# Expert 0's second 128 rows: half of their product before the attention branch ends, half behind it

## The chip, the cores and the metric

The kernel runs on one core of one Trainium2 chip. The metric is device time in microseconds of one execution. The kernel before takes 646.89 us (median of three runs, 646.09 to 647.37).

## The reference

Three stages follow each other, all in float32. `_attn_ref` is cut to its result, since the change touches only how its output is handed on.

```python
def reference(**kwargs):
    attn_out = _attn_ref(**attn_kwargs)             # B, H, S, D = 2, 8, 768, 64: local and global keys, ALiBi
    x = attn_out.transpose(0, 2, 1, 3).reshape(B, S, H * D)
    x = _moe_ref(x=x, **moe_kwargs)
    return _moe2_ref(x=x, **moe2_kwargs)

def _moe_ref(x, w_gate, w_local, w1, w2):           # E = 8 experts, D = 512, F = 1024
    logits = np.einsum('bsd,de->bse', x, w_gate)
    local_gate = 1.0 / (1.0 + np.exp(-np.einsum('bsd,de->bse', x, w_local).squeeze(-1)))
    for b in range(B):
        prev_e = -1
        for s in range(S):
            fresh_e = int(np.argmax(logits[b, s]))
            e = fresh_e if s == 0 or local_gate[b, s] < 0.5 else prev_e   # else: the expert of the token before
            prev_e = e
            p = softmax(logits[b, s])
            out[b, s] = p[e] * (np.maximum(x[b, s] @ w1[e], 0.0) @ w2[e])

def _moe2_ref(x, w_ch1, w_ch2):                     # FFT over sequence and channels, layer norm, a ReLU layer pair
    ...
```

## The kernel before, in words

**Stages.** The program runs attention and routing (to about 124 us), the eight experts (to about 318), and the mixer (FFT and a ReLU layer pair). Attention has two arms of one branch on the data (`tc.If(fast > 0)`): the fast arm runs here, and the code of the other, longer arm lies behind it, so that every engine jumps over it at the branch's end.

**Products in two halves.** TensorE takes each float32 operand as a high part (`h`, rounded) and the residual (`l`); a product is the sum of three: high by high, high by low, low by high. ScalarE makes the high part and VectorE the residual. A layer of 128 rows is 24 matmuls of 512 columns.

**Attention** goes over six tiles of 128 positions, four units each. `step(k)` runs between the parts of a unit; it takes one step of each background generator and, by the table `AHEAD`, some steps of the early product. `k` counts from the last unit, so `k >= 0` is the tail, in which only outputs and routing are left.

**Routing** (`Route.run`, one generator for each tile) finds each token's expert: `gn` and `gf` (line 528 and 534) are turned by TensorE, a scan carries the expert along (`ex`, line 552), a second scan counts (`cu`, line 561), `rk` (577) and `pos` (589) are the token's place. Then SP's queue writes the tokens to `xs` and GpSimd scatters their numbers to `list`, where each expert has its own part. Two `yield from to(...)` set at which part of a unit a step is taken; the last tile has none, so its steps follow `step(k)` one by one.

**The early product.** After the third tile (`first`), `less` pads expert 0's count to 128, so that the first 128 places of its list are settled; its entries are read (line 604) and its rows gathered to `x0` (607). `early` (862) is a generator that runs the two layers for these 128 rows (chunk 0) in the tail of attention: transposes of `x0` (868), first layer (882), copies of the sums to `hs` (885), `turned` (887: transposes, relu, residual), second layer (898), scaling (913). Its operands `xe`, `he` lie in a weight place (slot 4), its sums in the last raw place.

**The experts.** `Ring` holds four raw places, each for a piece of 1 MB, and six slots for their two halves; `take` splits a piece and loads the next one into its raw place. `Ring.shade` sets the order of the pieces: for each expert the next expert's four (`e`), and eight mixer pieces (`d`) in between, each decoded by VectorE in four instructions. `Moe.run` (1359) begins behind the branch: entries and rows of expert 0's other two chunks (1 and 2), the write of chunk 0's result, the counts (1371), 6 + 6 + 3 matmuls on a zero tile (`WARM`), the transposes of the two chunks. `expert(0)` then runs the first layer on 256 rows at once (`first256`, line 1201) and the second layer on each 128 (`second`, 1181). Chunk 0 of every other expert is part of its own 256 rows.

Of the kernel before, what the change touches and what calls it, by code (L numbers as in the profile page):

```python
# [60 lines left out]
def fast_attention(tc, st, io, route):  # L61
# [4 lines left out]
    with ExitStack() as ctx:  # L66
# [68 lines left out]
        def rowmin(n):  # L135
# [3 lines left out]
            for k in range(2):  # L139
                for j in range(2):  # L140
                    x = 2 * k + j
                    V.tensor_tensor_reduce(  # L142
                        out=u.t[:, x, :u.W], in0=u.sp[:, j, k, :u.W], in1=bias[:, 4 * u.g + x, u.b0:u.b0 + u.W],
                        scale=-0.125, scalar=3.0e38, op0=ALU.add, op1=ALU.min,
                        accum_out=u.nm[:, x:x + 1])
# [62 lines left out]
        bias = res.tile([P, H, 384], F32, name="bias")  # L208
# [44 lines left out]
        kept = []  # L253

        def spare():
            if not kept:
                kept.append(ps_s.tile([P, 2, 2, 256], F32, name="sp"))
            return kept[0]

        def places():  # L260
            for n in range(6):
                if n == 1:
                    yield spare()[:, 0].rearrange("p u n -> p (u n)")
                elif n in (2, 4):
# [4 lines left out]
        ahead = early(nc, st, places())  # L269

        def step(k):
# [13 lines left out]
            if k in SPIN:  # L285
                keep_busy(nc, st, spare()[:, 1].rearrange("p u n -> p (u n)"), SPIN[k])
# [62 lines left out]
def general_attention(tc, st, io, route):  # L349
# [3 lines left out]
    with ExitStack() as ctx:  # L353
# [74 lines left out]
        for _ in early(nc, st, (ps_s.tile([P, 1024], F32, name="sp")[:, :DM] if n in (2, 4) else ps_o.tile([P, DM], F32, name="op") for n in range(6))):  # L428
            pass
# [20 lines left out]
class Route:  # L450
# [31 lines left out]
    def run(self, i, xs, parts=None):  # L482
# [85 lines left out]
        if first:  # L568
# [6 lines left out]
        if soon:  # L575
            yield from to(1)
# [3 lines left out]
        yield from to(3, 2)  # L580
# [9 lines left out]
        for b in range(B):  # L590
            r = (i * B + b) * P
            nc.sync.dma_start(st.xs[r:r + P], xs[b])
            w = G.indirect_dma_start(
# [4 lines left out]
        if first:  # L598

            V.tensor_scalar(su[:1, 0], less, 0.0, None, op0=ALU.max)  # L600
            V.tensor_tensor(cu[:1, P - 1:], cu[:1, P - 1:], su[:1, 0], op=ALU.add)
            for _ in range(EARLY_READ):
                yield
            nc.sync.dma_start(st.ent0, st.list[1:P + 1])
            for _ in range(EARLY_GATHER):
                yield
            G.indirect_dma_start(
                out=st.x0, out_offset=None, in_=st.xs[:(i + 1) * B * P], in_offset=bass.IndirectOffsetOnAxis(ap=st.ent0[:, 0:1], axis=0),
                bounds_check=(i + 1) * B * P - 1, oob_is_err=False)
        if i == NT - 1:  # L610
            yield from self.counts()

# [42 lines left out]
EARLY_READ = 7  # L655
EARLY_GATHER = 6
# [3 lines left out]
WARM = 6, 6, 3  # L660
LOAD = 6
CASTS = (5, 6, 7, 8)
RESTS = (24, 25, 26, 27)
# [1202 lines left out]
```

## Time and profile before

| | |
|---|---|
| median of three runs | 646.89 us (646.09 to 647.37) |
| the profiled execution, in all | 645.5 us |
| its span, first to last instruction | 643.7 us |
| mean granted TensorE clock | 0.995 |
| TensorE busy (matmul) | 622.1 us, 97% of the span |
| VectorE busy | 391.7 us, 61% |
| ScalarE busy | 276.3 us, 43% |
| first product of expert 0's 256 rows | 129.86 us |
| first product of expert 1 | 153.30 us |

The profile calls the engines PE (TensorE), DVE (VectorE), ACT (ScalarE), POOL (GpSimd) and SP. Times in it are microseconds from the span's start. A share of busy time is a mean over stages; what a change in one stage is worth is read from that stage. Matmuls are pipelined: the time from one's start to the next one's start is what it costs, and is shorter than its own duration.

### The profile page before, as it was taken

To read this page: it belongs to the slowest core of one execution; us is meant where nothing else is said; L and a number is where in the kernel's file an instruction comes from. 1 tells how busy PE (TensorE), PEld (TensorE's weight loads), DVE (VectorE), ACT (ScalarE), POOL (GpSimd) and SP (SyncE) were. 2 spreads that over 40 slices of the span, in tenths; PEclk is the share of its full clock that TensorE was granted. 3 is DMA by queue.
4 is the path that set the end of the run, shared out by engine and by line. 5 is a ranking of instruction groups with operands and counts; after the bars stand their busy time and mean duration, and the time that the engine had idled before them with its cause. 6 is when DMAs were issued, how large, how long until landed. Compare 5 with 4: busy or idle time off the path is not lost.

```text
span 643.7 us, 9990 instructions
## 1 busy us (share of the span) xinstructions
PE 622.1 (97%) x3634; PEld 506.6 (79%) x3635; DVE 391.7 (61%) x904; ACT 276.3 (43%) x550; POOL 100.6 (16%) x146
## 2 busy tenths in 40 slices
PE   8999998899999999999999899999999999999997
PEld 4777875599899899887866787777788888888885
DVE  5788886379785988651489887898531220263112
ACT  5789883266475567552443534431121221041110
POOL 2126562312333034310100000000000000000000
PEclk8999999999999999999999999999999999999999
DMA  8356575358887978961450333451100010100001
GB/s 302 151 204 135 135 155 200 76 199 311 329 315 251 310 278 318 385 209 63 155 210 0 131 132 127 142 189 67 61 5 1 5 62 0 66 0 1 0 1 65
DMA packets 25187, 92.45 MB, mean 144 GB/s; under 512 B 7644, under 2 KB 8796, under 8 KB 17184
## 3 DMA queue, kind: packets, MB, share of 16 engines
q1 hardware_dynamic: 19664, 79.50, 36.8%
q0 software_dynamic: 4736, 10.56, 4.5%
q10 hardware_dynamic: 720, 1.55, 0.7%
q8 instruction: 35, 0.57, 0.3%
q14 instruction: 32, 0.26, 0.2%
HBM read 81.00 MB, written 14.84 MB: 149 GB/s over the span
## 4 chain that ended last, share of the span: by engine, by line
PE 39%; DVE 11%; ACT 2%; issue 1%; DMA 1%; DVEq 0%; ACTq 0%
PE h L1678 17%; PE acc L1694 6%; PE acc L1692 6%; PE acc L1693 6%; DVE dec L1072 1%; DVE dec L1074 1%; PE y L1181 1%; PE more L1231 1%; PE more L1181 1%; PE h L1231 1%; DVE dec L1070 1%; DVE dec L1068 1%; DMA u<-x 1%; PE f L1644 1%; DVE wide L1014 1%
## 5 line engine op out<-in xcount | busy, mean ns | idle before, releaser
L1683 DVE SCALAR_TENSOR_TENSOR hl<-h,hh 128x512 fp32r<-128x512 f32 x48 | 33.1, 690 | 118.4 <-ACT hh L1682 118.4
L1682 ACT ACTIVATE hh<-h 128x512 fp32r<-128x512 f32 x48 | 28.7, 598 | 153.7 <-PE h L1678 153.6
L1036 DVE TENSOR_TENSOR wide<-raws,wide 128x1024 fp32r<-128x1024 f32 (+1 forms) x38 | 45.0, 1201 | 24.3 <-ACT wide L1034 24.3
L151 ACT ACTIVATE t<-t,nm 128x256 f32<-128x256 f32 (+1 forms) x96 | 45.8, 478 | 10.5 <-DVE nm L142 10.5
L1034 ACT CAST wide<-raws 128x1024 fp32r<-128x1024 f32 (+2 forms) x42 | 40.9, 990 | 5.3 <-PE acc L1694 3.4
L1678 PE MATMUL h<-un0h,wide 128*128 128x512 f32 (+1 forms) x136 | 42.4, 378 | 0.1
L1693 PE MATMUL acc<-wide,hh 128*128 128x512 f32 x96 | 37.7, 393 | 0.0
L1692 PE MATMUL acc<-wide,hh 128*128 128x512 f32 x96 | 37.7, 393 | 0.0
L1694 PE MATMUL acc<-wide,hl 128*128 128x512 f32 x96 | 37.5, 391 | 0.0
L142 DVE CUSTOM_DVE_ANT_0 t<-sp,bias 128x256 f32<-128x256 f32 (+1 forms) x96 | 33.0, 398 | 7.0 <-PE sp L133 3.8
L1111 POOL DMA_INDIRECT xg<-xs,ent x23 | 27.8, 1209 | 14.1 <-issue 5.8
L1204 ACT ACTIVATE hh<-h 128x512 fp32r<-128x512 f32 x28 | 16.7, 598 | 29.1 <-PE h L1201 26.9
L1678 PEld LDWEIGHTS h<-un0h,wide 128*128 128x128 f32 x136 | 25.0, 188 | 5.0 <-ACT un0h L1454 0.3
L1201 PE MATMUL h<-xh,wide 128*128 128x256 f32 x192 | 28.4, 284 | 0.1
L161 PE MATMUL tp<-consts,t 128*128 128x128 f32 x176 | 26.3, 286 | 0.8 <-ACT p L167 0.7
L1201 PEld LDWEIGHTS h<-xh,wide 128*128 128x128 f32 x192 | 25.5, 192 | 0.9 <-issue 0.5
L161 PEld LDWEIGHTS tp<-consts,t 128*128 128x128 f32 x176 | 19.4, 142 | 8.5 <-ACT p L167 3.7
L1678 PE MATMUL h<-un0l,wide 128*128 128x512 f32 (+1 forms) x68 | 25.6, 377 | 0.0
L175 PE MATMUL sm<-p,vs 128*64 128x128 f32 x352 | 25.0, 283 | 0.0
L1205 DVE SCALAR_TENSOR_TENSOR hl<-h,hh 128x512 fp32r<-128x512 f32 x28 | 19.2, 686 | 9.2 <-ACT hh L1204 7.0
L167 ACT COPY p<-tp 128x512 f32<-128x512 f32 (+1 forms) x48 | 24.1, 535 | 0.8 <-PE tp L161 0.8
L1074 DVE SCALAR_TENSOR_TENSOR dec<-raws,dec 128x1024 int32<-128x1024 int32 x18 | 22.1, 1225 | 0.6
(460 smaller groups left out, 1651.6 us busy)
## 6 DMA issues: line engine op xcount, KB each, us to landing
raws<-we SPq DMA_DIRECT2D x31, 1024.0 KB, 8.9
raws<-wm SPq DMA_DIRECT2D x18, 1024.0 KB, 4.9
raws<-wmf SPq DMA_DIRECT2D x7, 1024.0 KB, 7.5
wmf<-dec POOLq DMA_DIRECT2D x8, 512.0 KB, 8.3
xs<-xrow SPq DMA_DIRECT2D x12, 260.0 KB, 6.5
vs<-v SPq DMA_DIRECT2D x6, 512.0 KB, 4.0
raws<-kq SPq DMA_DIRECT2D x3, 1024.0 KB
u<-x SPq DMA_DIRECT2D x6, 512.0 KB
```

What stands on the lines that cost most here:

```text
L142: V.tensor_tensor_reduce(out=u.t[:, x, :u.W], in0=u.sp[:, j, k, :u.W], in1=bias[:, 4 * u.g + x, u.b0:u.b0 + u.W], scale=-0.125, scalar=3.0 ...
L151: A.activation(u.t[:, x, :u.W], u.t[:, x, :u.W], AF.Exp, bias=u.nm[:, x:x + 1], scale=-1.0, accum_out=u.den[:, x])
L161: T.transpose(u.tp[k][:, j, c], u.t[:, 2 * k + j, c * P:(c + 1) * P], st.ident)
L1034: (first or nc.scalar.copy)(hi[:, cs], raw[:, cs])
L1036: (eng() if callable(eng) else eng or nc.vector).tensor_tensor(lo[:, cs], raw[:, cs], hi[:, cs].bitcast(F32), op=ALU.subtract)
L1201: T.matmul(ps[:, u], w[:, f], x[:, k], start=n == 0, stop=n == 11)
L1678: nc.tensor.matmul(ps[:, c], a[:, k], x[:, k, c], start=n == 0, stop=n == 11)
L1682: nc.scalar.activation(hh, ps, AF.Relu)
L1683: nc.vector.scalar_tensor_tensor(hl, ps, 0.0, hh.bitcast(F32), op0=ALU.max, op1=ALU.subtract)
L1692: T.matmul(acc[c], hh[:, cs], h2, start=first, stop=False)
L1693: T.matmul(acc[c], hh[:, cs], l2, start=False, stop=False)
L1694: T.matmul(acc[c], hl[:, cs], h2, start=False, stop=last)
```

## The change

Expert 0's second 128 rows (chunk 1) become an early product too. After the fifth tile (`soon`) its count is padded to 256, its entries are read and its rows gathered. `both` runs chunk 0's product, and after 42 of its steps starts chunk 1's: transposes, then the first layer behind chunk 0's last product. The branch ends there. `Moe.run` goes on with chunk 1's second layer, turns chunk 2's rows beside it, and writes the result; `expert(0)` has one chunk of 128 rows left, in 24 matmuls of 512 columns for each layer. The filling matmuls (`WARM`) are gone. The early operands move from slot 4 to the `bias` table and `vs`, and expert 1's first piece is split into slot 4 before the branch ends, its second beside chunk 1's second layer. `SHADE` gives the mixer pieces to the experts by hand: 0, 1, 2, 2, 2, 1, 0 in place of 2, 1, 1, 2, 1, 1, 0. `AHEAD` takes more early matmuls in each step, and the steps of tile 4's routing stand closer.

```diff
-        if first:
+        if first or soon:
             less = sm[:1, 6:7]
...
         if last:
             yield
-        if soon:
-            yield from to(1)
         V.scalar_tensor_tensor(rk, cu, other, oh, op0=ALU.add, op1=ALU.mult)
...
-        yield from to(3, 2)
+        yield from to(0 if soon else 3, 2)
...
-        if first:
-
-            V.tensor_scalar(su[:1, 0], less, 0.0, None, op0=ALU.max)
+        if first or soon:
+
+            V.tensor_scalar(su[:1, 0], less, float(P if soon else 0), 0.0, op0=ALU.add, op1=ALU.max)
             V.tensor_tensor(cu[:1, P - 1:], cu[:1, P - 1:], su[:1, 0], op=ALU.add)
-            for _ in range(EARLY_READ):
+        if first or soon:
+            n = int(soon)
+            for _ in range(EARLY_READ[n]):
                 yield
-            nc.sync.dma_start(st.ent0, st.list[1:P + 1])
+            nc.sync.dma_start(st.ents[n], st.list[1 + n * P:1 + n * P + P])
...
-EARLY_READ = 7
-EARLY_GATHER = 6
+SHADE = 0, 1, 2, 2, 2, 1, 0
+EARLY_READ = 7, 4
+EARLY_GATHER = 6, 9
...
-WARM = 6, 6, 3
-LOAD = 6
+OVER = 42
+TURN = 6
+LOAD = 2
...
-RESTS = (24, 25, 26, 27)
+RESTS = (10, 13, 19, 24)
...
+def both(nc, st, places, between=lambda: None):
+
+    one, two = early(nc, st, places, 0), early(nc, st, places, 1)
+    for _ in range(OVER):
+        yield next(one)
+    between()
+    for _ in range(2):
+        yield next(two)
+    yield from one
+    piece = st.ring.take("e", PIECES, follow=False)
+    for n, _ in enumerate(two):
+        if n % 4 == 3:
+            next(piece, None)
+        yield
...
-        if n == 22:
+        if n == 22 and not part:
             turned(0)
         yield
+    if part:
+        return
...
-            self.first256(e, lambda: bg.step(2) if e or next(calls) > 1 else None)
+            if e:
+                self.first256(e, step)
+            else:
+                late = self.first128(w1, *self.more, (self.ps_h, "h"), spare, step)
...
-        keep_busy(nc, st, spare, WARM[0])
         counts = nc.values_load(st.nch[0:1, E + 1:E + 2], min_val=0, max_val=2 * 4 ** E - 1)
-        keep_busy(nc, st, spare, WARM[1])
-        for _ in self.tokens(0):
-            pass
-        keep_busy(nc, st, spare, WARM[2])
-        ring.load(2 * PIECES - 1, nc.scalar)
+        spare = self.ps_more, "more"
+        hs = [st.hs[1][:, u * DM:u * DM + DM] for u in range(2)]
+        self.turned(hs, self.more[1], spare, 0)
+        ring.load(2 * PIECES)
+        bg = Background()
+        bg.add(ring.take("e", PIECES + 1))
+        calls = iter(range(8))
+
+        def step():
+            n = next(calls)
+            if n == 1:
+                ring.load(2 * PIECES - 1)
+            if n == TURN:
+                bg.add(self.turn(2, 0, self.place(0, 2)))
+            bg.step()
+
+        y = self.second(*self.more[1], rows(st, 2), *spare, step, lambda: self.turned(hs, self.more[1], spare, 1))
+        self.write(y, st.p[1], st.ents[1][:, 1:2], "ys")
+        bg.drain()
+        self.weight(0, (2,))
```

VectorE in the last tile's routing, the kernel before: from the first scan (L552) to `pos` (L589).

```order
L552 SCALAR_TENSOR_TENSOR ex<-rows,ex,sm 16x128
L555 RECIPROCAL su<-su 128x2
L557 TENSOR_SCALAR oh<-ex,consts 16x128
L561 SCALAR_TENSOR_TENSOR cu<-consts,cu,oh 16x128
L577 SCALAR_TENSOR_TENSOR rk<-cu,sm,oh 16x128
L579 TENSOR_SCALAR xrow<-pe,su 128x8 x2
L589 CAST pos<-sm 128x2
```

The same place now; L931 is the residual of `turned`, whose result lies in what was `bias`, and L1092 the residual of a weight piece's quarter.

```order
L555 SCALAR_TENSOR_TENSOR ex<-rows,ex,sm 16x128
L558 RECIPROCAL su<-su 128x2
L560 TENSOR_SCALAR oh<-ex,consts 16x128
L931 SCALAR_TENSOR_TENSOR bias<-tp,bias 128x512
L564 SCALAR_TENSOR_TENSOR cu<-consts,cu,oh 16x128
L1092 TENSOR_TENSOR wide<-raws,wide 128x512
L578 SCALAR_TENSOR_TENSOR rk<-cu,sm,oh 16x128
L580 TENSOR_SCALAR xrow<-pe,su 128x8 x2
L931 SCALAR_TENSOR_TENSOR bias<-tp,bias 128x512
L590 CAST pos<-sm 128x2
```

Two residuals of the early product and one of a weight piece moved in between the routing's steps.

TensorE at the same place now: the end of chunk 0's first layer (L920), `turned(0)` (L928), the two products of the counts (L569, L570), `rk` (L582).

```order
L920 MATMUL sp<-sl0h,bias 128x512 x2
L920 MATMUL sp<-sl1h,bias 128x512
L928 MATMUL tp<-consts,vs 128x128 x4
L569 MATMUL sm<-cu,consts 16x1
L570 MATMUL sm<-cu,consts 16x1
L920 MATMUL sp<-sl1h,bias 128x512
L937 MATMUL sp<-wide,bias 128x512
L582 LDWEIGHTS rk
```

Before, these products stood among the first layer's first half of matmuls, ahead of any `turned`.

ScalarE's last rows in the fast arm, before: copies of the sums (L885), relus (L892), the scaling of the result (L913), the branch.

```order
L885 COPY raws<-sp 128x512
L892 ACTIVATE wide<-tp 128x512
L885 COPY raws<-sp 128x512
L892 ACTIVATE wide<-tp 128x512
L913 ACTIVATE raws<-sp,p_90 128x512
L1839 UNCONDITIONAL_BRANCH
```

ScalarE's last rows in the fast arm now: chunk 1's tokens (L908), chunk 0's scaling (L954), expert 1's first piece (L1075), the copies of chunk 1's sums (L923).

```order
L908 CAST bias<-tp 128x512
L954 ACTIVATE raws<-sp,few 128x512
L1075 CAST wide<-raws 128x1024 x2
L923 COPY raws<-tp 128x512
L923 COPY raws<-sp 128x512
L1900 UNCONDITIONAL_BRANCH
```

And its first rows behind the branch now: the load of the counts (L1417), the relus of chunk 1 (L1255), expert 1's second piece, chunk 2's tokens (L1186).

```order
L1417 TENSOR_LOAD nch
L1255 ACTIVATE hh_6426<-more 128x512
L1075 CAST sl5h<-raws 128x1024
L1255 ACTIVATE hh_6426<-more 128x512
L1075 CAST sl5h<-raws 128x1024
L1186 CAST xh_6440<-more 128x512
```

Before, the first row behind the load of the counts was the cast of chunk 1's gathered tokens (L1146); now a relu of chunk 1 stands there, and its input is the copy just ahead of the branch.

## Rows read from the trace of the kernel before

**Rows 1.** The page's slices: granted TensorE clock in 40 slices, tenths.

```profile
PEclk8999999999999999999999999999999999999999
```

**Rows 2.** TensorE's waits from 129 to 320 us: total us, times, longest.

```profile
PE more L1231 <- ACTq L1335: 0.8, 1, 0.8
```

**Rows 3.** A stretch: length; busy PE, PEld, DVE, ACT, POOL; clock; DMA; GB/s.

```profile
200.80:224.50 23.70, 23.55 (x154) 21.35 (x153) 20.33 (x25) 14.49 (x18) 5.20 (x5) 1.00 0.78 258
```

**Rows 4.** Timeline, TensorE: start, us, operation; in brackets the idle time before.

```profile
103.68 0.49 PE L882 MATMUL sp<-sl0h,wide 128*128 128x512 f32 x1 [0.68 <-ACT wide L870]
104.10 1.09 PE L175 MATMUL sm<-p,vs 128*64 128x128 f32 x16
...
119.23 4.83 PE L898 MATMUL sp<-wide 128*128 128x512 f32 x20
124.79 2.76 PE L50 MATMUL more<-busy 128*128 128x512 bf16 x12 [0.73 <-PE sp L898]
...
129.86 0.39 PE L1201 MATMUL h<-xh,sl0h 128*128 128x256 f32 x1
...
153.30 0.64 PE L1201 MATMUL h<-xh,wide 128*128 128x256 f32 x4
```

**Rows 5.** The chain that ended last, in the last expert: start, us, piece.

```profile
300.41 0.44 PE more L1220 x4
300.85 4.36 PE more L1181 x19
```

**Rows 6.** Timeline, the last tile's routing on VectorE and TensorE.

```profile
108.41 0.18 DVE L534 SCALAR_TENSOR_TENSOR gf<-lg,fr 128x16 bf16<-128x16 f32 x1
108.64 0.22 PE L538 MATMUL sm<-identb,gf 128*16 128x128 bf16 x1 [0.47 <-DVE gf L534]
110.28 0.47 DVE L561 TENSOR_TENSOR_SCAN cu<-consts,cu,oh 16x128 f32<-16x128 f32 x1
110.80 0.20 PE L567 MATMUL sm<-cu,consts 16*16 16x1 f32 x2 [0.66 <-DVE cu L561]
111.67 0.16 DVE L589 CAST pos<-sm 128x2 int32<-128x2 f32 x1
```

**Rows 7.** Timeline, `turned(0)`: transposes, relu, residual.

```profile
116.21 0.66 PE L890 MATMUL tp<-consts,raws 128*128 128x128 f32 x4 [0.26 <-ACT raws L885]
116.90 0.60 ACT L892 ACTIVATE wide<-tp 128x512 fp32r<-128x512 f32 x1 [0.75 <-PE tp L890]
117.58 0.67 DVE L893 SCALAR_TENSOR_TENSOR wide<-tp,wide 128x512 fp32r<-128x512 f32 x1
```

**Rows 8.** Timeline, GpSimd and SP: last list write, entries, first gather.

```profile
113.59 0.97 POOL L593 DMA_INDIRECT list<-dest,pos  x1 [0.30 <-issue]
118.83 2.99 SPq L1127 DMA_DIRECT2D ent<-list  x3
123.04 1.07 POOL L1111 DMA_INDIRECT xg<-xs,ent  x1 [2.74 <-DMA ent<-list]
```

**Rows 9.** Timeline, three engines at the branch's end.

```profile
119.29 1.00 POOL L1108 MEMSET xg<- 128x520 f32 x2 [4.73 <-issue]
120.14 0.69 DVE L893 SCALAR_TENSOR_TENSOR wide<-tp,wide 128x512 fp32r<-128x512 f32 x1 [1.89 <-ACT wide L892]
123.78 1.04 DVE L1365 MEMSET xg<- 128x520 f32 x2 [2.95 <-issue]
124.14 0.69 ACT L913 ACTIVATE raws<-sp,p 128x512 f32<-128x512 f32 x1 [4.04 <-PE sp L898]
128.42 0.59 ACT L1146 CAST xh<-xtp 128x512 fp32r<-128x512 f32 x1 [3.58 <-DMA x<-raws,ent]
```

**Rows 10.** Stretches of a microsecond, TensorE; the third number from the end is its clock.

```profile
112.00:113.00 1.00, 1.00 (x4) 0.50 0.64 243
...
114.00:115.00 1.00, 1.00 (x4) 0.50 0.37 9
```

**Rows 11.** The page's DMA issues: count, us from issue to landing.

```profile
xg<-xs,ent POOLq DMA_INDIRECT x23, 4.6
```

More of the change, by code (lines that the diff above doesn't have):

```diff
@@ L267, in places @@
                     yield ps_t.tile([P, 2, 2, P], F32, name="tp").rearrange("p a b n -> p (a b n)")
-        ahead = early(nc, st, places())
+        rooms(st, bias.rearrange("p h n -> p (h n)"), vs[:, 0].rearrange("p h d -> p (h d)"))
+        ahead = both(nc, st, places())
         def step(k):
@@ L427, in general_attention @@
                 pass
-        for _ in early(nc, st, (ps_s.tile([P, 1024], F32, name="sp")[:, :DM] if n in (2, 4) else ps_o.tile([P, DM], F32, name="op") for n in range(6))):
+        rooms(st, one.tile([P, 6 * DM], F32R, name="early"), one.tile([P, 2 * DM], F32, name="rows"))
+        wide = lambda: ps_s.tile([P, 1024], F32, name="sp")[:, :DM]
+        for _ in both(nc, st, (wide() if n % 6 in (2, 4) else ps_o.tile([P, DM], F32, name="op") for n in range(12)), lambda: route.rows(1, NT - 1)):
             pass
@@ L592, in run @@
             nc.sync.dma_start(st.xs[r:r + P], xs[b])
+        for b in range(B):
             w = G.indirect_dma_start(
@@ L1150, in tokens @@
         for c in range(2):
-            yield from self.turn(e % 2, c, self.place(e, c + (e == 0)))
+            yield from self.turn(e % 2, c, self.place(e, c))
             yield
-        self.weight(e, range(2) if e else (1, 2))
+        self.weight(e, range(2))
     def weight(self, e, cs):
@@ L1273, in third @@
                 result(2, self.more[1], spare, "more", lambda: None, late)
-        first, then = ([ring.take(*u, follow=e < LAST) for u in units] for units in ring.plan[e])
+        first, then = ([ring.take(*u, follow=e < LAST) for u in units if u not in (("e", PIECES), ("e", PIECES + 1))] for units in ring.plan[e])
         if e < LAST:
@@ L1287, in expert @@
             bg.add(chain(*then))
+            if e == 0:
+                result(2, self.more[1], spare, "more", step, late)
+                return
             own = lambda c: [t[0][:, :, c * P:(c + 1) * P] for t in (self.hh, self.hl)]
-            result(at, own(0), (self.ps_y, "y"), "ys", step)
-            with tc.If(n > at + 1):
-                result(at + 1, own(1), spare, "more")
+            result(0, own(0), (self.ps_y, "y"), "ys", step)
+            with tc.If(n > 1):
+                result(1, own(1), spare, "more")
             return
```

117 lines of the change are left out of this document (64 added, 53 removed).

## The prediction

> **What bounds the kernel now.** I read the views in this order. First the page's slices: the clock is at its full level in nearly every slice [rows 1], so the time is made of TensorE's work and its waits. Then what TensorE waited for from 129 to 320 us, which is the whole of the eight experts: one wait of 0.8 us [rows 2]. There TensorE is never idle, so whatever brings the first product of expert 1 (153.30) forward or back moves everything behind it by as much, as long as nothing behind it becomes late. Its stretch with the most VectorE work, with two mixer pieces in one expert, had VectorE busy 20.33 of 23.70 us [rows 3]; that is the cover for the moved pieces. Then TensorE's own timeline at the handover [rows 4]: the early product of expert 0's first 128 rows begins at 103.68 and ends at 124.06 (119.23 + 4.83); from 124.79 fifteen matmuls on a zero tile fill the wait for the gathered rows; 129.86 is the first product of expert 0's other 256 rows, 153.30 that of expert 1. So 49.6 us lie between the first early product and expert 1, 5.8 of them with no useful work on TensorE, and inside the rest there are more waits (0.47, 0.66 in the last tile's routing [rows 6]). What can be won lies there.
>
> **The change part by part.** *Work.* One 512-column matmul costs 0.23 us (4.36 over 19), four transposes 0.44 [rows 5]. Between the first early product and expert 1 the changed kernel has six products of 24 matmuls (first and second layer of three chunks of 128 rows): 144 x 0.23 = 33.1. It has eight groups of transposes behind the first product (0.44 each, 3.5), two for expert 1's rows (0.9), 0.6 for the last attention output and 0.4 of small routing matmuls: 38.5 us. The sixteen value matmuls now stand ahead of the first product instead of behind it (104.10 to 105.13, 1.0 [rows 4]), and `rk` and the two `xrow` products of tile 4 ahead of the copy that the next output waits for (0.2 more), so that it begins near 104.9. With no wait expert 1 would begin at 104.9 + 38.5 = 143.4, 9.9 us sooner. The old 256-row product and the fifteen filling matmuls are gone, and both are in the 49.6.
>
> *Waits that the new order makes.* (1) VectorE has the residual of the first chunk's tokens and a 512-column residual of a weight piece ahead of `gf`, 0.67 each (one of that size stands in [rows 7]), less 0.1 since the tile begins a little earlier; `gf`'s product stood at 108.64 [rows 6] and comes to 109.8. TensorE has reached it at 108.6: 1.2 us. (2) The order shows `turned(0)`'s residual on VectorE ahead of the scan `cu`. That residual needs ten more matmuls (to 112.2), the transposes and ScalarE's relu; from the transposes to the start of the residual took 117.58 - 116.21 = 1.37 [rows 7], partly at the low clock, so 1.3. It runs 113.5 to 114.2, `cu` follows, and 0.52 later (110.28 to 110.80 [rows 6]) its product, at 114.7. TensorE, which has only that product left in its queue's order, waits from 112.7: 2.0 us. (3) `rk` then waits for one more weight residual: 0.3. Behind (3) stands `pos`, after the second `turned` as well: 114.8, plus 0.6 for the matmuls and the wait for `rk`, 0.7 for three more matmuls, 2.0 for transposes, relu and residual gives 118.3, where it was 111.67 [rows 6], 6.6 us later.
>
> (4) That delays chunk 2's rows. From `pos` to the gather's issue it took 123.04 - 111.67 = 11.4 us (list write, entries, gather [rows 8]), and a gather lands 4.6 later [rows 11]: 134.3. They are wanted after 21 matmuls of chunk 1's second product, which is 137 below. So this has 3 us in hand, and I cost it at nothing; if the wait (5) is not there, it is what comes late next.
>
> (5) The branch's end. In the kernel before VectorE issued its last operation in the branch at 120.14 and its next one, two memsets, at 123.78, 3.64 later, although GpSimd's memset, which waits for the same list writes and token writes and for more, started at 119.29 [rows 9]. The trace names no work that ended that idle time. ScalarE's last operation of the branch began at 124.14 and its first behind it at 128.42, 4.28 later [rows 9], with the load of the counts between them; it also waited for transposes there, so 4.28 is the upper bound of its crossing, and nothing the lower one. I take 4.28, since VectorE's bare 3.64 is near it. Before, TensorE lost nothing by ScalarE's, as it was waiting for rows. Now ScalarE's last operation in the branch is the copy of the last sum of chunk 1's first layer, and its first behind it is the relu that TensorE's next product reads. Five waits, 114.8 + 49 matmuls (11.3) + two transposes (0.9) + 0.3 puts the last of these sums at 127.3; 4.28 more is 131.6, and 0.6 for the relu [rows 7] lets TensorE go on at 132.2. It has its four transposes meanwhile, so the wait is 4.4 us. The Trainium skill has this as a rule (Runtime: NRT & Kernel Launch, Instruction fetch mechanics): a taken branch whose target lies outside the engine's sequential window has to fetch the code there first. By that rule every engine pays at this branch whatever its work, the trace agrees for VectorE with 3.64 us between two issues, and the rule speaks against a product that stands on both sides of a branch's end. Without such a fetch the sum would be that of rival B.
>
> (6) Expert 1's first gather is issued behind the write of chunk 1's result. By the same sums its rows land about when TensorE wants them: 0 to 0.5, I take 0.2.
>
> From 132.2: 72 matmuls (16.5) + six groups of transposes (2.7) + 0.2 = 151.6 for expert 1, against 153.30: **-1.7 us**.
>
> *The clock.* Before, in 112 to 115 the granted clock was 0.50, the low level of 1.2 GHz (three rows of a microsecond [rows 10]), after the waits for `gf` and `cu` [rows 6]. Such a stretch of 3.3 us costs about 1.6. The new wait of 4.4 us is longer than all of these, so I count one such stretch behind it: **+1.6**. Waits (1) and (2) replace the old ones in the tail; whether the clock falls there too is a rival.
>
> *At nothing.* The two mixer pieces taken from expert 0 go to experts 2 and 4, which then have two: VectorE did that in expert 3 with 3.4 us to spare [rows 3]. The weight load that ScalarE's queue issued at 129.9 now stands on SP's queue behind the one for raw place 0, and waits for the early result to be written out (about 135); it is wanted near 145, and the load queued behind it later. The third of the early loads is another piece of the same size, and the list's padding for tile 4 is two instructions of one element on VectorE, ahead of any wait. If the load were 4 us late, ScalarE's casts would hold expert 1's relu by what exceeds 2 us.
>
> **The rivals.**
> *A, slower:* the clock falls in the tail as well. For it: waits (1) and (2) are 3.2 us within 108.6 to 114.7, and 1.1 before were enough [rows 6, 10]. Against it: between them the products are dense, where before they were spread. Price another 1.6, total +1.5 (0.7 to 2.5 with a late gather of chunk 1's rows, which the new order leaves no slack either): 648.4. It decides if the low clock stands both in 110 to 120 and behind the branch.
> *B, faster:* ScalarE's crossing is covered, since its code is there when it arrives. Then (5) and the fall behind it vanish, -6.0, but TensorE comes to chunk 2's rows at 133.6 while they land at 134.3, +0.7 to 1.5: 642.2, or 641.5 to 643.2. For it: ScalarE's 128.42 was also waiting for transposes [rows 9]. Against it: VectorE waited 3.64 with nothing to wait for.
> *C, the gain does not arrive:* two mixer pieces in three experts running, or the late loads, hold a residual or a relu and TensorE waits there, 1 to 3 us: 648 to 650. Against it: 3.4 us to spare in [rows 3] and no wait in 190 us [rows 2].
>
> **How the numbers follow.** The sum is made on the profiled execution (span 643.7, 645.5 in all, 1.4 below the median of the runs). -1.7 + 1.6 = -0.1, on the median 646.89: 646.8. Forecast 0.41 with its own range of 645.3 to 648.0 (each wait within 0.5), A 0.25, B 0.26, C 0.08. Both signs are in play, so the range runs from B's middle to just past A's: 642.2 to 648.9. About 0.2% (1.3 us) is what a measurement of this kernel can tell from no change. Faster by more: B and a fifth of the forecast, 0.34. Slower by more: a little of the forecast, most of A, most of C, 0.28. The rest is 0.38.
>
> **What would show it.** (1) to (3): TensorE waits of 1 and 2 us for `gf` and `cu`, `pos` near 118. (5): ScalarE's relu about 4.3 after the last copy of the branch, TensorE idle from 127.8 to 132.2; a shorter gap is B. The clock: low rows behind that gap alone, or in the tail too (A). Expert 1's first product at 153 +- 1.5. It is wrong if that product and the end move apart (C), if `pos` comes before 115, or if chunk 2's rows hold TensorE.

## The result, and the profile after

| | before | after |
|---|---|---|
| median of 12 runs, us | 647.12 (644.87 to 649.68) | 653.5 (648.72 to 659.16) |
| ratio | | 1.0079, 95% interval 1.0053 to 1.0105 |
| profiled execution, us | 645.5 (span 643.7) | 648.72 (span 647.0) |
| expert 1's first product, us | 153.30 | 153.46 |
| expert 6's first product, us | 267.09 | 269.14 |

The changed kernel is 0.8% slower, about 5 us. The ratio is one of means, and leaves out one of the changed kernel's twelve executions, 659.16 us, that fell in the chip's slower state; the medians lie 6.4 us apart. The forecast was 646.8 with a range of 642.2 to 648.9: both its sign of no change and its range failed. The execution that was profiled is the shortest of the twelve, so its trace shows only 3.2 of the 5 us; where the rest is became clear only from further profiles.

First the waits of TensorE from 129 to 320 us in the changed kernel (total us, times, longest), the answer to [rows 2], where one wait of 0.8 us stood:

```profile
PE more L1221 <- ACT hh L1255: 3.2, 1, 3.2
PE h L1241 <- DVE hl L1245: 1.7, 2, 1.4
PE xtp L1183 <- DMA xg<-xs,few: 0.9, 2, 0.6
PE more L1275 <- ACTq L1383: 0.8, 1, 0.8
```

The first is the wait behind the branch. The second and third are new and lie in experts 5 and 6, about 95 and 130 us behind everything that the prediction worked out step by step; the fourth is the wait of 0.8 us that stood there before. Next the timeline of TensorE at the handover and at the first products of experts 1, 4, 5 and 6 (the answer to [rows 4, 6]):

```profile
103.17 0.50 PE L920 MATMUL sp<-sl0h,bias 128*128 128x512 f32 x1
...
107.88 0.22 PE L541 MATMUL sm<-identb,gf 128*16 128x128 bf16 x1 [0.77 <-DVE gf L537]
...
113.06 0.20 PE L570 MATMUL sm<-cu,consts 16*16 16x1 f32 x2 [1.66 <-DVE cu L564]
...
125.83 0.63 PE L920 MATMUL sp<-sl1h,bias 128*128 128x512 f32 x2
127.55 0.63 PE L1253 MATMUL more<-consts,raws 128*128 128x128 f32 x4 [1.08 <-ACT raws L923]
131.34 2.50 PE L1221 MATMUL more<-wide,hh 128*128 128x512 f32 x5 [3.16 <-ACT hh L1255]
...
153.46 0.64 PE L1241 MATMUL h<-xh,wide 128*128 128x256 f32 x4
...
224.63 0.64 PE L1241 MATMUL h<-xh,wide 128*128 128x256 f32 x4
243.23 1.19 PE L1241 MATMUL h<-xh,wide 128*128 128x256 f32 x8
250.54 1.23 PE L1241 MATMUL h<-xh,wide 128*128 128x256 f32 x8 [1.38 <-DVE hl L1245]
269.14 0.28 PE L1241 MATMUL h<-xh,sl0h 128*128 128x256 f32 x1
```

Expert 1 begins 0.16 us later than before, and so does expert 5 (243.23 against 243.08). Expert 6 begins 2.05 later, expert 7, behind the wait for its rows, 3.43 later (289.11 against 285.68), and the end is 3.2 later. So in this execution the handover, which the whole forecast was about, cost nothing and gained nothing, and the loss is made in experts 5 and 6.

The branch's end on the other engines, and `pos` (the answer to [rows 6, 8, 9]):

```profile
116.72 0.15 DVE L590 CAST pos<-sm 128x2 int32<-128x2 f32 x1
122.56 2.36 DVE L1077 TENSOR_TENSOR wide<-raws,wide 128x1024 fp32r<-128x1024 f32 x2 [2.10 <-ACT wide L1075]
129.76 1.04 DVE L1413 MEMSET xg<- 128x520 f32 x2 [4.84 <-issue]
```

```profile
126.55 0.59 ACT L923 COPY raws<-sp 128x512 f32<-128x512 f32 x1 [0.35 <-PE sp L920]
130.69 0.60 ACT L1255 ACTIVATE hh<-more 128x512 fp32r<-128x512 f32 x1 [3.56 <-issue]
```

From ScalarE's last start in the branch to its first behind it are 4.14 us; it then lets TensorE go on at 131.34. And the clock, in stretches of a microsecond (length; busy PE, PEld, DVE, ACT, POOL; clock; DMA share; GB/s; the answer to [rows 10]):

```profile
129.00:130.00 1.00, 0.00 (x0) 0.00 (x0) 0.23 (x1) 0.00 (x0) 0.79 (x1) 0.94 0.93 393
130.00:131.00 1.00, 0.00 (x0) 0.00 (x0) 0.75 (x2) 0.31 (x1) 0.00 (x0) 0.50 1.02 406
...
136.00:137.00 1.00, 1.00 (x4) 0.76 (x4) 1.00 (x2) 0.26 (x1) 0.00 (x0) 0.65 0.46 164
```

It is at the low level of 1.2 GHz from 129.9 to 136.7, from inside the wait to 5.4 us behind it, and at the full level in the routing tail of this execution, where it was low before.

### The profile page after: what moved, and what is told of

It is laid out like the page before. It is cut to its first block, busy times and chain, and to the rows that moved or that the text cites. A ratio compares the mean times of both kernels' runs of the same rounds, so it can differ in the third digit from the quotient of the medians.

```text
span 647.0 us, 9888 instructions
## 1 busy us (share of the span) xinstructions
PE 619.9 (96%) x3591; PEld 504.9 (78%) x3592; DVE 391.9 (61%) x906; ACT 278.6 (43%) x554; POOL 99.6 (15%) x146
## 5 line engine op out<-in xcount | busy, mean ns | idle before, releaser
L1744 DVE SCALAR_TENSOR_TENSOR hl<-h,hh 128x512 fp32r<-128x512 f32 x48 | 33.1, 690 | 118.4 <-ACT hh L1743 118.4
L1743 ACT ACTIVATE hh<-h 128x512 fp32r<-128x512 f32 x48 | 28.7, 598 | 153.3 <-PE h L1739 153.2
L1075 ACT CAST wide<-raws 128x1024 fp32r<-128x1024 f32 (+2 forms) x42 | 40.8, 990 | 10.6 <-DMA raws<-we 6.5
L1151 POOL DMA_INDIRECT xg<-xs,few x22 | 25.8, 1171 | 9.6 <-issue 5.8
L1244 ACT ACTIVATE hh<-h 128x512 fp32r<-128x512 f32 x24 | 14.4, 599 | 23.1 <-PE h L1241 23.1
L167 ACT COPY p<-tp 128x512 f32<-128x512 f32 (+1 forms) x48 | 24.1, 536 | 0.3 <-PE tp L161 0.3
L1100 ACT ACTIVATE dec<-raws 128x1024 f32<-128x1024 f32 x18 | 20.7, 1152 | 6.7 <-DMA raws<-wm 2.1
L1115 DVE SCALAR_TENSOR_TENSOR dec<-raws,dec 128x1024 int32<-128x1024 int32 x18 | 22.0, 1225 | 0.6
```

What stands on the lines that cost most here:

```text
L1075: (first or nc.scalar.copy)(hi[:, cs], raw[:, cs])
L1743: nc.scalar.activation(hh, ps, AF.Relu)
L1744: nc.vector.scalar_tensor_tensor(hl, ps, 0.0, hh.bitcast(F32), op0=ALU.max, op1=ALU.subtract)
```

## Experiments

Where a table or sentence gives a ratio, it is to the kernel before on the same chip.

| kernel | median us (before) | ratio (95%) | expert 1 | expert 5's length |
|---|---|---|---|---|
| before | 647.12 | 1 | 153.30 | 24.0 |
| after | 653.5 (647.12) | 1.0079 (1.0053 to 1.0105) | 153.46 | 25.9 |
| again | one run, 650.32 | | 153.58 | 28.7 |
| shade4 | 649.03 (647.77) | 1.0006 (0.9976 to 1.0035) | 155.57 | 24.9 |
| warm | 651.29 (647.77) | 1.0062 (1.0027 to 1.0098) | 151.86 | 30.2 |
| before_shade | 648.79 (647.77) | 1.0019 (0.9998 to 1.0040) | 157.32 | 26.1 |
| shade6 | 647.67 (647.60) | 0.9994 (0.9969 to 1.0019) | 157.96 | 24.9 |
| warm6 | 646.71 (647.60) | 0.9979 (0.9943 to 1.0015) | 155.83 | 24.1 |
| end6 | 644.13 (644.89) | 0.9982 (0.9971 to 0.9994) | 151.02 | 23.7 |
| end | 651.09 (646.42) | 1.0073 (1.0048 to 1.0099) | 152.51 | 29.6 |
| late8 | 647.75 (646.87) | 1.0009 (0.9979 to 1.0040) | 155.24 | 24.6 |
| shade6_again | 647.37 (646.87) | 1.0002 (0.9972 to 1.0032) | 155.95 | 23.9 |
| cu | one run, 655.09 | | 156.41 | 30.5 |
| vcopy | one run, 651.15 | | 153.58 | 29.4 |
| noload | one run, 650.75 | | 155.43 | 26.4 |
| nodec | one run, 656.11 | | 157.58 | 29.7 |

Expert 1 is the start of its first product, and expert 5's length is from its own first product to expert 6's, both in the profiled execution. Ratios are of means and the column beside them has medians, so the two need not agree to the last tenth of a per cent.

**Where the other executions lose.** The changed kernel, unaltered:

> The changed kernel once more, nothing altered. Its median of 653.5 lies 4.8 above the execution that was profiled (648.72, span 647.0, clock 0.993), and most of its other executions have a mean clock of 0.985 to 0.987. If those have one more stretch at the low clock and the same waits, a profile of about 652 to 655 shows expert 1's first product later than 153.46 by 2 to 5 us, or low rows somewhere else, and the same shifts behind expert 1 (2.0 at expert 5's end). If they have other waits, the row that grew shows where.

Its waits from 120 to 320 us, and ScalarE's timeline ahead of the longest:

```profile
PE h L1241 <- DVE hl L1245: 3.2, 1, 3.2
PE more L1221 <- ACT hh L1255: 2.1, 1, 2.1
PE more L1253 <- ACT raws L923: 1.7, 1, 1.7
```

```profile
245.11 1.15 ACT L1100 ACTIVATE dec<-raws 128x1024 f32<-128x1024 f32 x1 [1.62 <-DMA raws<-wm]
246.16 0.68 ACT L1203 ACTIVATE ys<-y,few 128x512 f32<-128x512 f32 x1
249.57 1.05 ACT L1075 CAST sl0h<-raws 128x1024 fp32r<-128x1024 f32 x1 [2.73 <-DMA raws<-we]
250.52 0.59 ACT L1244 ACTIVATE hh<-h 128x512 fp32r<-128x512 f32 x1
```

The low stretch and the grown row are in expert 5: its wait is 3.2 us, not 1.4, and the clock is low behind it (0.50 from 253 to 256). ScalarE stands at a cast that waits 2.73 us for its load, and the relu that TensorE needs is queued behind that cast. Expert 5 takes 28.7 us instead of 24.0. Every later kernel with the changed kernel's deal of pieces and with all of that deal's loads shows the same, waits of 3.7 to 4.4 us and a length of 29.4 to 30.5. So the profiled execution of the changed kernel was the exception: in the six other profiles with these loads expert 5 loses 4.7 to 6.5 us, not 1.9.

**The pieces.** Edits of one line, first in the changed kernel, then in the kernel before:

```diff
-SHADE = 0, 1, 2, 2, 2, 1, 0
+SHADE = 0, 2, 2, 2, 1, 1, 0      (shade4)
+SHADE = 0, 1, 2, 2, 1, 1, 1      (shade6)
...
-            for _ in range(-(-min(e + 1, E - 2) * 2 * EARLY // (E - 2)) + -min(e, E - 2) * 2 * EARLY // (E - 2)):
+            for _ in range((2, 1, 1, 1, 2, 1, 0)[e]):      (before_shade)
```

> The changed kernel with its mixer pieces dealt 0, 2, 2, 2, 1, 1, 0 over the experts instead of 0, 1, 2, 2, 2, 1, 0: expert 4 has one piece again, as before the change, and expert 1 has two. Theory (expert 4 is only 18.6 us long and cannot hide a second piece): TensorE's wait of 1.4 us for a residual in expert 5 and the wait of 0.9 us for expert 7's rows go, the end stands 3 us sooner against expert 1 than in the changed kernel, and the time falls by 2.5 to 3.3 us. Rival (it is the number of pieces behind expert 0 that costs, wherever they stand): a wait of 1 to 2 us stands behind expert 1 or 3 instead, and the time stays within 1 us of the changed kernel's.

> The kernel before with its mixer pieces dealt 2, 1, 1, 1, 2, 1, 0 instead of 2, 1, 1, 2, 1, 1, 0: the second piece of expert 3 goes to expert 4, and nothing else is altered. Theory (a second piece in expert 4 costs 3 us): the time rises by 2.5 to 3.3 us with a wait of some 1.5 us in expert 5 and one of some 0.9 us ahead of expert 7. Rival (expert 4 hides it, and the waits in the changed kernel came from its late loads in expert 0): within 0.7 us of the kernel before.

> The changed kernel with its mixer pieces dealt 0, 1, 2, 2, 1, 1, 1: the second piece of expert 4 goes to expert 6, and nothing else is altered. Theory (expert 4, 18.6 us long, cannot hide two pieces, and the run of 0, 2, 2, 2 pieces left 0.9 us of the wait because the loads ran late): the wait in expert 5 falls under 0.3 us, no low clock follows it, and the time lies 3 to 5 us under the changed kernel's, at the kernel before's or up to 1 us above. Rival (the loads behind expert 0 are late whatever expert 4 does): a wait of 1 us or more stays in expert 5.

Taking the second piece from expert 4 takes the loss away: the ratio falls from 1.0079 to 1.0006 and to 0.9994 (1.0002 when it was run again), so 4.7 to 5.5 us, more than shade4's expected 2.5 to 3.3, which came from the profiled execution alone. In the kernel before, a second piece in expert 4 costs 1.2 us by the ratio, whose interval just reaches 1, with waits of 1.05 us in expert 5 and 0.76 ahead of expert 6: the waits are there, the size is under the expected 2.5 and not clear of noise. There one piece each stood in the two experts ahead; in the changed kernel two each did. shade4, with three experts of two pieces in a row, kept a wait of 0.9, shade6 one of 1.0 in one profile and none over 0.15 in the other.

Expert 1's 157.32 in before_shade's profile, the slowest of its ten executions, lies ahead of what the edit touches: there TensorE stood 1.5 and 2.0 us behind the branch for nothing that the trace names. So the kernel before, too, does not always start expert 1 at 153.30.

Why expert 4: it is short. (Expert 6 is as short, and held its one piece in shade6.) Stretches from the first product of expert 4 to that of expert 5, before and after, and one expert of two pieces, expert 3 (columns as above):

```profile
224.48:243.08 18.60, 18.30 (x129) 16.70 (x128) 15.70 (x21) 12.69 (x16) 6.51 (x7) 1.00 0.82 292
```

```profile
200.90:224.63 23.73, 23.58 (x153) 21.36 (x152) 20.36 (x26) 14.51 (x18) 6.71 (x7) 1.00 0.90 321
224.63:243.23 18.60, 18.30 (x130) 16.70 (x128) 16.00 (x21) 12.80 (x16) 6.33 (x7) 1.00 0.88 301
```

The stretch that the prediction took as cover [rows 3] is 23.70 long. Expert 4's is 18.60, and VectorE was busy 15.70 of it with one piece; a second one, 3.9 us on VectorE (L1109 to L1115), does not fit in the 2.9 left, and the load of 1 MB comes on top.

**Load or VectorE?** Each of two kernels takes one half of the piece away, and leaves the other:

```diff
+            k = P if n == 6 else PW                         (noload)
-            (queue or nc.sync).dma_start(t.bitcast(I32), io["wm"][n].bitcast(I32))
+            (queue or nc.sync).dma_start(t.bitcast(I32)[:, :k], io["wm"][n].bitcast(I32)[:, :k])
...
-            for k, _ in enumerate(self.bits(words, t)):     (nodec)
+            for k, _ in enumerate(self.bits(words, t) if n != 6 else range(4)):
```

> The changed kernel with the load of mixer piece 6 (the second of expert 4) cut to a sixteenth of its columns; its four steps on VectorE, its step on ScalarE and its write stay, on what lies in the place, so that part of the mixer's weights is not the reference's. Theory (expert 4 is bound by the bytes that its loads move: six pieces of 1.05 MB, two writes of half that and 1.3 MB of rows at the 420 GB/s of the full stretches are 20.6 us, and it is 18.6 us long): the wait in expert 5 falls from 1.4 to 4.4 us to under 0.7, with no low clock there. Rival (VectorE cannot fit the second piece's four steps, 3.9 us): the wait stays over 1.3 us.

> The changed kernel with the load of mixer piece 6 whole, and its four steps on VectorE (3.9 us) left out, so that part of the mixer's weights is not the reference's. Theory (bytes): the wait in expert 5 stays over 1.3 us, since ScalarE's cast ahead of the relu still waits for its load. Rival (VectorE): it falls under 0.7 us.

TensorE's waits from 120 to 320 us without the load, and without VectorE's steps:

```profile
PE more L1222 <- ACT hh L1256: 2.4, 1, 2.4
PE more L1254 <- ACT raws L923: 1.4, 1, 1.4
PE h L1242 <- DVE hl L1246: 1.4, 1, 1.4
```

```profile
PE more L1221 <- ACT hh L1255: 6.5, 1, 6.5
PE h L1241 <- DVE hl L1245: 4.3, 1, 4.3
```

Without the steps nothing is won, 4.3 us. Without the load 1.4 us stay, with no low clock; VectorE has no idle time there from 244.5 to the residual that TensorE waits for, with the four steps in between. So neither theory is whole: VectorE's steps are not what makes the wait of 3 to 4.4 us, and where the load is out of the way they still hold expert 5 by 1.4. That the load makes the rest is likely and not shown: it rests on one profile, and the changed kernel with its load had 1.4 in one of its two. The sum of bytes in the expectation (20.6 us of moving) overstates it: the DMA engines were at 0.88 over expert 4, not full.

**The wait behind the branch.** Three edits: 13 matmuls on a zero tile in the wait (warm), chunk 1's sums copied by VectorE, with its two memsets behind the first residual (vcopy), and one early step moved so that the scan stands ahead of the residual (cu).

```diff
         self.turned(hs, self.more[1], spare, 0)
+        keep_busy(nc, st, self.ps_h.tile([P, 512], F32, name="h"), 13)      (warm)
...
-                    A.copy(hs[:, f], ps[u])
+                    (V.tensor_copy if part else A.copy)(hs[:, f], ps[u])    (vcopy)
...
-AHEAD = dict(enumerate([1, 1, 0, 4, 3, 2, 2, 2, 4, 2, 2, 1, 1, 0, 2, 0, 0, 2, ...
+AHEAD = dict(enumerate([1, 1, 0, 4, 3, 2, 2, 2, 4, 2, 2, 1, 0, 0, 3, 0, 0, 2, ...      (cu)
```

> The changed kernel with 13 matmuls on a zero tile behind the four transposes that open chunk 1's second layer, in the place where TensorE waited 3.16 us for ScalarE to come out of the branch; their result is read by nobody. Theory (the low clock from 129.9 to 136.6 follows that wait and doubles the 5.3 us of work in it): the clock stays at full level, expert 1's first product comes 2.5 us sooner, and so does the end. Rival (the clock falls for the first wait, 1.1 us at the branch, or for the sparse stretch ahead of it): low rows remain and the time changes by under 0.7 us.

```profile
131.94 1.44 PE L1221 MATMUL more<-wide,hh 128*128 128x512 f32 x5
```

The clock stays at 1.00 in every stretch there, and from the transposes behind the branch to expert 1 are 23.1 us (128.72 to 151.86) instead of 25.9: 2.8 us. Not all of that is the clock: ScalarE's relu came 0.6 us sooner after the transposes in this execution. From TensorE's first product behind the wait to expert 1 are 19.9 us (from 131.94) instead of 22.1 (131.34 to 153.46, and 22.1 in again too): the low stretch costs 2.2. The time falls by 1.1 us by the ratios, whose intervals overlap, so no gain in time is shown; expert 5's length is 30.2 us in this profile.

> The changed kernel with chunk 1's two sums copied out by VectorE instead of ScalarE, and VectorE's two memsets behind the first residual. So ScalarE's last work in the branch ends near 123.5 instead of 127.1, and VectorE's near 127.2. Theory (an engine pays 3.5 to 4.8 us from its last work in the branch to its first behind it, each on its own): ScalarE is across at about 127.5 and its relu follows the transposes at once, at 128.3 instead of 130.7; VectorE is across at 130.8 to 132, and TensorE waits 0.3 to 1.5 us for the residual instead of 3.2 for the relu. Expert 1 starts 2 to 3.5 us sooner, more if the clock holds. Rival (ScalarE is held behind the branch by something that ends at 130.7 for all engines): the relu stays near 130.7 and nothing is won.

```profile
130.64 0.60 ACT L1255 ACTIVATE hh<-more 128x512 fp32r<-128x512 f32 x1 [5.27 <-PE more L1253]
131.29 2.50 PE L1221 MATMUL more<-wide,hh 128*128 128x512 f32 x5 [0.74 <-ACT hh L1255]
147.40 0.65 PE L1183 MATMUL xtp<-consts,xg 128*128 128x128 f32 x4 [1.10 <-DMA xg<-xs,few]
```

ScalarE, done with the branch at 125.4, follows the transposes at once, and TensorE waits 0.74 for it, not 3.16. VectorE crosses, which is to say stands idle over the branch's end, in 3.1 (129.09 to 132.21). Expert 1 comes 23.7 us after the transposes instead of 25.9; a new wait of 1.1 for its own rows is in that. It comes no sooner in all (153.58), since the transposes begin at 129.92 in this execution. So each engine pays for the branch on its own, and from its own last work there.

> The changed kernel with the last tile's scan ahead of chunk 0's first residual on VectorE, and its product ahead of the transposes on TensorE, by moving one early step (AHEAD ..., 1, 1, 0, 2 to 1, 0, 0, 3); nothing else. Theory (TensorE's wait of 1.66 us is that of the scan behind the residual): the wait is gone; in its place TensorE waits at the start of chunk 0's second layer for ScalarE's relu, 0.5 to 1 us, and expert 1 starts 0.6 to 1.2 us sooner. Rival (the scan was late for another reason): a wait of over 1 us stays ahead of the scan's product.

The scan's wait went, as said, and two others took its place, 0.46 for the relu and 1.08 for `rk`, together 1.54 for 1.66: nothing won. Expert 1 came at 156.4, and not 0.6 to 1.2 sooner as expected, because ScalarE's crossing was 6.2 us there; kernels without this edit show such a crossing too.

**Both together, and the branch's end moved.** warm6 is the deal of shade6 with the 13 matmuls. end6 leaves of chunk 1 only the transposed tokens in the branch; its first layer stands behind it:

```diff
+    if part:
+        V.tensor_tensor(xl, tp, xh.bitcast(F32), op=ALU.subtract)
+        V.tensor_copy(p, st.x0[:, DM:DM + 1])
+        return
...
-        self.turned(hs, self.more[1], spare, 0)
-        ring.load(2 * PIECES)
+        late = self.first128(rows(st, 0), st.x1, self.more[1], (self.ps_h, "h"), spare)
```

> Both edits together: pieces dealt 0, 1, 2, 2, 1, 1, 1, and the 13 matmuls on a zero tile behind the branch. Theory (the two costs, 2.6 us of clock at the handover and 3 to 5 us in experts 4 to 7, are separate): expert 1's first product 2.6 us sooner than in the run with the pieces alone, and so is the end; 644.5 to 646.5, faster than the kernel before by 1 to 2 us. Rival (a sooner start of expert 1 makes its loads late, as the wait in expert 5 grew from 1.4 to 3.7 us when only the matmuls were added): expert 1 starts sooner, a wait grows behind it, and the time stays within 0.7 us of the run with the pieces alone.

> Pieces dealt 0, 1, 2, 2, 1, 1, 1, and the branch's end moved ahead of chunk 1's first layer: of chunk 1 only the transposed tokens are made inside the branch, and the cast of weight piece 4, whose place they lie in, goes behind it, into expert 0. ScalarE's and VectorE's last work in the branch then ends near 121.6 and 120.4, and 24 matmuls of TensorE stand between that and the first thing it needs of them, instead of none. Theory (what the change lost at the handover is the crossing of the branch by ScalarE and VectorE, 3 us or 6 us from run to run, plus the clock behind it): TensorE waits for its own crossing, 1 to 1.7 us, for chunk 2's rows 0 to 2 us, and little else; no low clock from 128 to 140; expert 1 starts at 148 to 150 instead of 153.5 to 158, and the time falls to 642 to 644.5. Rival (TensorE will wait for whatever comes across last, rows of chunk 2 above all, and the clock falls there): expert 1 starts at 151.5 or later, and the time is that of the matmul fill, 646 to 647.

> The branch's end ahead of chunk 1's first layer, as in the run that had it with the pieces dealt 0, 1, 2, 2, 1, 1, 1, but with the changed kernel's own 0, 1, 2, 2, 2, 1, 0. Theory (two separate costs): expert 1 starts near 151, without a low clock ahead of it, expert 5 has a wait of 3 to 4.5 us with a low clock behind it, and the time is 4 to 6 us above that run's against the kernel before, a ratio of 1.004 to 1.008. Rival (the loads were late because the start behind the branch was): the wait in expert 5 is under 1 us and the ratio under 1.001.

warm6: ScalarE's crossing was 5.4 us in the profile, so the 13 matmuls ran out and 2.6 us of wait were left; 646.71 us, just above the expected 644.5 to 646.5, and 0.9979, whose interval holds 1. end6, TensorE's waits from 120 to 320 us and ScalarE at the branch's end:

```profile
PE h L1272 <- issue: 2.6, 1, 2.6
PE xtp L1180 <- DMA xg<-xs,few: 0.8, 1, 0.8
PE more L1272 <- ACTq L1380: 0.8, 1, 0.8
```

```profile
121.91 0.69 ACT L951 ACTIVATE raws<-sp,few 128x512 f32<-128x512 f32 x1 [1.34 <-PE sp L936]
127.57 0.59 ACT L1277 COPY dec<-h 128x512 f32<-128x512 f32 x1 [4.98 <-PE h L1272]
```

ScalarE is waiting for TensorE and not the other way round; TensorE's wait is its own crossing, 2.6 us where 1 to 1.7 were expected, so that expert 1 comes at 151.0 and not at 148 to 150. The time is 0.18% under the kernel before, the only kernel here whose interval lies below 1, and its ten executions lie within 641.7 to 644.9. Its 644.13 us are inside the expected 642 to 644.5 by luck: the kernel before took 644.89 beside it, not 647, so the gain is 1.2 us and not the 2.5 to 5 that was meant. end, the same with the changed kernel's own deal, starts expert 1 at 152.5 and loses everything again in expert 5: 1.0073. So the two costs are separate.

**What makes a crossing long?** In seven profiles ScalarE's idle time behind the branch, up to that relu, was 2.9 to 3.6 us, in four 5.4 to 6.3. The DMA engines' busy share over that idle time, in 40 slices, in the changed kernel (127.1 to 130.7) and in shade6 (129.9 to 136.0):

```profile
DMA  3000300696990078650920992696299089469909
```

```profile
DMA  9597979798987999897592402002010100000020
```

```profile
129.28 0.59 ACT L923 COPY raws<-sp 128x512 f32<-128x512 f32 x1 [0.35 <-PE sp L920]
136.02 0.60 ACT L1255 ACTIVATE hh<-more 128x512 fp32r<-128x512 f32 x1 [6.16 <-issue]
```

In the long ones (shade6, cu, warm6, nodec) the DMA engines are full for the first half and quiet for the last 2 to 3 us; the sync engine had issued a 1 MB load 2.2 us before ScalarE's last work in the branch ended, in the short ones that have this load there, between 0.3 us before that and 0.3 behind. What the crossing waits for is in the traces as well: they list the packets of code that the DMA engines move, as kind `instruction`, and in all eleven profiles a pair of 8 KB on queue 14 comes around or behind the end of ScalarE's last work. The queue's line in the changed kernel from 127.13 to 128.0, and in shade6 from 132.6 to 133.3 (packets, MB, share):

```profile
q14 instruction: 2, 0.02, 7.4%
```

```profile
q14 instruction: 2, 0.02, 5.5%
```

In the seven short crossings the second packet of the pair starts 0.35 to 0.6 us after ScalarE's last work has ended, in the four long ones 2.0 to 3.1 us after it; in shade6 no packet of code moves from 129.86 to 132.6, while the load does. From the end of that packet to the relu it is 2.1 to 2.7 us in the short ones and 2.8 to 3.1 in the long ones. So the long crossings are those in which the code came late, with the DMA engines full of a load. late8 moves that load behind the one of piece 7:

```diff
-        ring.load(2 * PIECES)
...
                 ring.load(2 * PIECES - 1)
+                ring.load(2 * PIECES)
```

> The kernel with the pieces dealt 0, 1, 2, 2, 1, 1, 1, and the load of weight piece 8 called behind that of piece 7, which waits for the early result to be written out, instead of ahead of it: the sync engine's first 1 MB load behind the branch then starts near 135 and not at 126.4 to 129.7. Nothing else is altered. Theory (the crossing takes 3.0 to 3.6 us where that load was issued 0.3 to 0.6 us ahead of ScalarE's last work in the branch, and 5.4 to 6.6 where it was issued 2 us or more ahead, since the DMA engines are then full for the first half of it): the crossing takes 3.6 us at most and TensorE's wait behind the branch 3.2 us at most, in every execution, so the clock of the executions spreads less (0.990 to 0.997 instead of 0.986 to 0.997) and the median falls by 1 to 2.5 us against the same kernel with the early load. Rival (both lengths come from something else, and the load goes with it): crossings of over 5 us still occur and median and spread stay.

> The kernel with the pieces dealt 0, 1, 2, 2, 1, 1, 1 once more, on the same chip as the run with the late load, to be compared with it: by the theory its executions fall in two groups, with crossings of 3 and of 6 us, and its median lies 1 to 2.5 us above; by the rival there is no difference.

In late8's profile the load starts at 136.8 and the crossing is short (3.1 us), but so it is in shade6_again's (2.9). The two are not alike, though: the sync engine's two reads of the lists, ahead of the load, take 0.82 us in late8 as in all four long crossings, and 2.8 to 3.6 in the other six short ones. Here in shade6, late8 and shade6_again:

```profile
124.44 0.82 SPq L1167 DMA_DIRECT2D few<-list  x2
```

```profile
125.44 0.82 SPq L1167 DMA_DIRECT2D few<-list  x2
```

```profile
126.02 3.59 SPq L1167 DMA_DIRECT2D few<-list  x2
```

So late8 had the start that led to a long crossing four times out of four, and without the load had a short one. This speaks for the load as the cause; it is one profile. Medians and spreads agree, 647.75 (645.05 to 652.62) against 647.37 (645.85 to 652.58), so the load is not what spreads the executions, and the expected 1 to 2.5 us did not come. Why the reads are short in one execution and long in another stays open.

## Why the prediction was wrong

*Waits (1) to (3).* Right in kind, 0.77 and 1.66 us for 1.2 and 2.0, none for 0.3. `pos` came at 116.72, for 118.3: the tail's clock stayed up in this execution, and the wait ahead of it was shorter.

*(4)* Chunk 2's rows held nobody, as costed. *(6)* Nothing, for 0.2.

*(5), the branch's end.* Right in place and size: 4.14 us from start to start for 4.28, the relu at 130.69 for 131.6, TensorE idle 1.08 and 3.16 for 4.4 in one piece. vcopy and end6 show that it is the crossing, engine by engine. That rival B (the code is there when the engine arrives) was out is settled by ScalarE's 3.56 us of idle time with a pair of code packets in it. This agrees with the rule of the Trainium skill (Runtime: NRT & Kernel Launch, Instruction fetch mechanics) that a taken branch to code outside the engine's window waits for a fetch. The runs have 2.9 to 6.3 us of idle time on ScalarE for the same two instructions. That spread was not foreseen, and that the profiled execution fell close to 4.28 is in part luck.

*The clock.* Right in kind, mis-sized: +1.6 was taken from a low stretch of 3.3 us; the new one lasts 6.8 us, 5.4 of them full of work, and warm shows 2.2 us. The shorter waits of the tail made up for it, and the handover's sum of -0.1 stands against a measured +0.16. That agreement is luck: errors offset each other, and in the seven profiles that have this handover unaltered expert 1 begins at 153.46 to 157.96, in five of them at 155.4 or later. For comparison there are only one profile of the kernel before and one of before_shade, with 153.30 and 157.32, so what the handover costs on the average is known from the ratios alone: about nothing, by shade4 and shade6.

*Rival A* (low clock in the tail too) did not happen in the changed kernel's two profiles, but it did in ten of the twelve profiles of other kernels with that tail (one of them with the scan moved), all but those of warm and end6, between 112 and 120 us and with the same waits of 0.8 and 1.7 us. So A, at 0.25, was too low; what decides is open, and it belongs to the spread. Rival B's range has a slip in its sum: -6.0 and +0.7 to 1.5 on 646.8 are 641.5 to 642.3, not up to 643.2. Nothing else hangs on it.

*"At nothing".* This is the step that failed. The prediction hid the two moved pieces under a stretch of 23.70 us [rows 3], that of an expert with three chunks, and let that stand for expert 4 too. The distance of first products in the trace of before, 224.48 to 243.08, is that of an expert of 18.60 us with 2.9 us of VectorE and 0.18 of the DMA engines free. It is rival C, which was given 0.08 and 1 to 3 us; in expert 5 it costs 1.9 us in the execution that was profiled and 4.7 to 6.5 in the six others; by the ratios of end (1.0073) and end6 (0.9982), which differ in the deal alone, it is 5.9. The sign that was named for it came: expert 1 and the end moved apart, by 0.16 and 3.2 us. The late load that C named as a cause is there, but of an expert a hundred microseconds on, where the prediction looked for it at the handover. Two errors of size follow from that one: the waiting cast stands ahead of a relu in ScalarE's queue, so a late load is a wait of TensorE; and the low clock stood at each of the six waits of 3.2 to 4.4 us in expert 5, while it stood at none of those of 0.6 to 1.4.

The sentence that a shift of expert 1 is a shift of the end "as long as nothing behind it becomes late" was the right frame; its condition was examined only on one engine and in one expert.

## What to carry to other kernels

Before background work is moved to "some later stage", list the length of every stage from the trace, and for the shortest one count each resource that the work takes: the vector engine, the DMA engines, the places that its load waits for, and what is queued behind a consumer that waits. Where a product straddles the end of a branch, give TensorE a stretch of its own work between the last thing the other engines do inside and the first thing it needs from them behind; that took the wait for ScalarE and VectorE away here, where filling the wait only kept the clock up. Profile more than one execution before a cause is named: the one profiled here was the fastest of twelve, and showed 1.9 us of a loss in expert 5 that was 4.7 to 6.5 in six other profiles, and a handover at the early end of its spread.

## What the runs showed of the hardware

The same two instructions on both sides of the branch's end had 2.9 to 3.6 us of idle time between them on ScalarE in seven profiles and 5.4 to 6.3 in four, with no edit that tells the two kinds apart; on VectorE in the same profiles it was 4.3 to 4.8 in the short and 6.9 to 8.2 in the long ones. The packets of code share the DMA engines with the loads, and the pair at the crossing moved 0.35 to 0.6 us after ScalarE's last work in the short ones and 2.0 to 3.1 us after it in the long ones, where a 1 MB load had been issued 2.2 us before that work ended. Thirteen matmuls on a zero tile, 2.97 us of them, held the clock at its full level through a wait that otherwise left it at half for 6.8 us, and saved 2.2 us up to expert 1 though nobody read their result.
